# One GpSimd drain in each expert unit of the second MoE, behind the unit's last gather from the result

## The chip, the cores and the metric

The kernel runs on one core of a Trainium2 chip. The metric is the device time in microseconds (us) of one execution; lower is better. The engines are named as in the profile: PE (TensorE), DVE (VectorE), ACT (ScalarE), POOL (GpSimd) and SP (SyncE). An engine's name with a q behind it (POOLq, SPq) is that engine's instruction sequencer, which handles semaphores, branches, drains and the issue of DMAs.

## The reference

```python
def reference(**kwargs):
    ...
    attn_out = _attn_ref(**attn_kwargs)            # local window plus block summaries, (2, 8, 768, 64)
    B, H, S, D = attn_out.shape
    x = np.ascontiguousarray(attn_out.transpose(0, 2, 1, 3)).reshape(B * S, H * D)
    x = _moe_ref(x=x, **moe_kwargs)                # leaky-ReLU feed-forward, 512 -> 2048 -> 512
    return _moe2_ref(x=x, **moe2_kwargs)

def _moe2_ref(x, w_gate, w_noise, noise, w1, w2):
    ...
    top2 = np.argpartition(-noisy_logits, 2, axis=1)[:, :2]     # two of 8 experts for each of 1536 tokens
    ...
    out = np.zeros((N, D), dtype=np.float32)
    for e in range(E):
        for k in range(2):
            mask = top2[:, k] == e
            ...
            h = np.maximum(x[mask] @ w1[e], 0.0)
            out[mask] += top2_w[mask, k, None] * (h @ w2[e])
    return out.astype(np.float32)
```

## The kernel before

The program has three parts. Attention and the first feed-forward layer fill about the first 430 us; a table of planned steps sets their order. During that time the router writes, for every token and each of its two experts, a row into a table in DRAM, by scatters of single rows (L531, 24 DMAs). All of that stays as it was.

The second MoE works through nine **units**: unit 0 and unit 1 are the two halves of expert 0's 420 slots, and units 2 to 8 are experts 1 to 7 with 420 slots each, in four pieces of 105 rows. For a unit, `gather` reads the unit's rows of the table, clamps the token numbers on POOL (`gi`, L763) and fetches the tokens with one indirect DMA per piece (`xg`, L770). `xg_t` transposes them on PE (L787). `m1` and `m2` are the two matrix products, eight slices each (L800, L819). Since every token has two experts, a unit adds to what is already in the result: `gather_acc` fetches the result's present rows by indirect DMA (`ag`, L777), and `finish` multiplies the product by the gate, adds `ag` on DVE (L857) and scatters the sum back to the result (L858). All these indirect DMAs are issued by POOL. Units 0 and 1 have nothing to add to, and `gather_acc` issues nothing for them.

The loop over a unit's eight slices is software-pipelined: `gather(u + 1)` stands in slice 0, the previous unit's `finish` in slices 2 and 3, and `gather_acc(u)` at the end of slice 3. On POOL the order that results in a middle unit is: four scatters (L858), four gathers from the result (L777), the clamp for the next unit (L763), four gathers of tokens (L770), and so on. ACT and DVE have a fixed order; PE and POOL take theirs from the scheduler.

Behind the last unit stands a branch for experts that have more tokens than slots (L982 and L983), which this input does not take. Then the program's context closes: all engines drain, meet at a barrier, and the semaphores are cleared. The profile shows these closing instructions at L1019, the opening ones at L1008. At the branch's end (L983) POOL's sequencer also executes one INC_SWDGE_SEM, which brings the semaphores of its DMA queue to the values that both ways through the branch agree on.

Of the kernel before, what the change touches and what calls it, by code (L numbers as in the profile page):

```python
# [18 lines left out]
IOA = bass.IndirectOffsetOnAxis  # L19
# [101 lines left out]
def attention_moe_kernel(ctx: ExitStack, tc: tile.TileContext, q, k, v, w_in, w_out, w_gate, w_noise, noise, w1, w2,  # L121
                         const, const_bf, out):
    nc = tc.nc
# [28 lines left out]
    def load_piece(e, i):  # L152

        m, c = i // 4 + 1, i % 4
        n = 4 * m
        if c == 0:
            ew[e, m] = tuple(t.rearrange("p (c f) -> p c f", c=n) for t in pair(f"e{e}{m}", e % 2))
        hi, lo = (t.rearrange("p c f -> p (c f)")[:, c * 1024:(c + 1) * 1024] for t in ew[e, m])
        raw = spool.tile([P, 1024], F32, tag="s4", name=f"e{e}{m}{c}")
        if m == 1:  # L160
            nc.sync.dma_start(raw, w1[e, c * P:(c + 1) * P, :])
        else:
            nc.sync.dma_start(raw.rearrange("p (c f) -> p c f", c=2),
                              w2[e, c * 256:(c + 1) * 256, :].rearrange("(c p) f -> p c f", p=P))
        split(hi, lo, raw, nc.vector)
# [592 lines left out]
    def gather(u):  # L758
        e, r0, nj = units[u]
        tb = rp.tile([SLOTS, nj, 2], I32, tag="tb", bufs=3, name=f"tb{u}")  # L760
        nc.sync.dma_start(tb, tabd[e * TS + r0:e * TS + r0 + nj * SLOTS, :].rearrange("(p j) c -> p j c", j=nj))
        gi = rp.tile([SLOTS, nj], I32, tag="gi", bufs=3, name=f"gi{u}")
        nc.gpsimd.tensor_scalar(gi, tb[:, :, 0], (N if u else N - G) - 1, None, op0=ALU.min)  # L763
        if u:
            x = mp.tile([SLOTS, nj, DM], F32, tag="xg", name=f"xg{u}")
        else:
            x = pa.tile([SLOTS, nj, DM], F32, tag="qn", bufs=1, name=f"xg{u}")
        xg = [x[:, j, :] for j in range(nj)]
        for j in range(nj):
            nc.gpsimd.indirect_dma_start(out=xg[j], out_offset=None, in_=x2d if u else x2d[:N - G, :], in_offset=IOA(ap=gi[:, j:j + 1], axis=0))  # L770
        ex[u] = dict(tb=tb, gi=gi, xg=xg, e=e, nj=nj, n=nj * SLOTS)

    def gather_acc(u):
        d = ex[u]
        d["ag"] = mp.tile([SLOTS, d["nj"], DM], F32, tag="ag", name=f"ag{u}")
        for j in range(d["nj"] if d["e"] else 0):
            nc.gpsimd.indirect_dma_start(out=d["ag"][:, j, :], out_offset=None, in_=out,  # L777
                                         in_offset=IOA(ap=d["gi"][:, j:j + 1], axis=0))

    def xg_t(u, c):  # L780
        d = ex[u]
        if c == 0:
            d["x"] = [(mp if u else pa).tile([P, KD, d["n"]], F32R, tag=f"x{s}0", name=f"ex{s}{u}") for s in "hl"]
        xh, xl = d["x"]
        ps = bank("VR"[c % 2], f"xgps{u}{c}")
        for j in range(d["nj"]):
            nc.tensor.transpose(ps[:, j * SLOTS:(j + 1) * SLOTS], d["xg"][j][:, c * P:(c + 1) * P], ident[:SLOTS, :SLOTS])  # L787
        nc.scalar.activation(xh[:, c, :], ps[:, :d["n"]], AF.Copy)
        nc.vector.tensor_sub(xl[:, c, :], ps[:, :d["n"]], xh[:, c, :].bitcast(F32))

    def m1(u, f):
        d = ex[u]
        wh, wl = ew[d["e"], 1]
        xh, xl = d["x"]
        w = d["n"]
        ps = bank("H%d" % (f % 2), f"eh{u}{f}")
        n = 0
        for c in range(KD):
            for a, x in ((wh, xh), (wh, xl), (wl, xh)):
                nc.tensor.matmul(ps[:, :w], a[:, c, f * P:(f + 1) * P], x[:, c, :], start=n == 0, stop=n == 3 * KD - 1)  # L800
                n += 1
        gh, gl = ((mp if u else pa).tile([P, w], F32R, tag="g" + s, bufs=3, name=f"eg{s}{u}{f}") for s in "hl")
        nc.scalar.activation(gh, ps[:, :w], AF.Relu)  # L803
        nc.vector.scalar_tensor_tensor(gl, ps[:, :w], 0.0, gh.bitcast(F32), op0=ALU.max, op1=ALU.subtract)  # L804
        d["g", f] = (gh, gl)
# [16 lines left out]
    def out_sb(u):  # L822
        d = ex[u]
        w = d["n"]
        for i in range(2):
            y = pa.tile([P, 2, w], F32, tag=f"x{'hl'[i]}0", name=f"y{u}{i}")
            for c in (2 * i, 2 * i + 1):
                copy(i, y[:, c % 2, :], d["acc", c])
                d["y", c] = y[:, c % 2, :]
# [13 lines left out]
    def finish(u, j, rows=False):  # L843

        d = ex[u]
        if rows:
            ps = d["acc", j]
        else:
            ps = bank("VR"[j % 2], f"yps{u}{j}")
            for c in range(KD):  # L850
                nc.tensor.transpose(ps[:SLOTS, c * P:(c + 1) * P], d["y", c][:, j * SLOTS:(j + 1) * SLOTS], ident)  # L851
        y = d["ag"][:, j, :]
        gate = d["tb"][:, j, 1:2].bitcast(F32)
        if d["e"] == 0:
            nc.vector.tensor_scalar(y, ps[:SLOTS, :], gate, None, op0=ALU.mult)
        else:
            nc.vector.scalar_tensor_tensor(y, ps[:SLOTS, :], gate, y, op0=ALU.mult, op1=ALU.add)  # L857
        i = nc.gpsimd.indirect_dma_start(out=out, out_offset=IOA(ap=d["tb"][:, j, 0:1], axis=0), in_=y, in_offset=None,  # L858
                                         bounds_check=N - 1, oob_is_err=False)
        for o in d.setdefault("out", []):  # L860
            tc.declare_no_dep(i.ins, o.ins, reason="an expert has each token once")
        d["out"].append(i)
# [25 lines left out]
    def second(u, f):  # L888
        if rows[u]:
            for j in range(units[u][2]):  # L890
                m2_rows(u, f, j)
        else:
            m2(u, f)
# [13 lines left out]
    second(0, 3)  # L907
    route_end()
    gather_acc(0)
    for f in range(5, NFE):  # L910
        m1(0, f)
# [6 lines left out]
    for u in range(1, nu):  # L918
        end = u == nu - 1
        for f in range(NFE):  # L920
            m1(u, f)
            if f == 0 and not end:
                gather(u + 1)
            if units[u][0] + 1 < E and f < 7:
                load_piece(units[u][0] + 1, f)
            if f == 1 and u > 1:
                second(u - 1, NFE - 1)
                if not rows[u - 1]:
                    out_sb(u - 1)
            if f in (2, 3) and u > 1:  # L930
                for j in range(2 * f - 4, min(2 * f - 2, units[u - 1][2])):
                    finish(u - 1, j, rows[u - 1])
            if f == 3:
                gather_acc(u)
            if f == NFE - 1 and not end:
                for c in range(2):
                    xg_t(u + 1, c)
            if f >= 2 and not (end and f == NFE - 1):
                second(u, f - 2)
        if not end:  # L940
            for c in range(2, KD):
                xg_t(u + 1, c)
            if units[u][0] + 1 < E:
                load_piece(units[u][0] + 1, 7)
            second(u, NFE - 2)
# [78 lines left out]
```

## Time and profile before

| what | us |
|---|---|
| median of 3 runs (lowest, highest) | 760.88 (760.31, 761.65) |
| the profiled execution, its own time | 759.27 |
| its span, first to last instruction | 757.5 |
| its mean granted TensorE clock, as a share of 2.4 GHz | 0.978 |

The span counts the sequencers' instructions too, so opening and closing work is in it. Semaphore waits, branches, drains and the issue of DMAs are never counted as an engine's busy time.

### The profile page before, as it was taken

How to read it: one execution, taken by the hardware profiler on the slowest of the kernel's cores; microseconds unless marked ns; L12 is line 12 of the kernel's file. 1: busy time of each engine (PE TensorE's matmuls, PEld its weight loads, DVE VectorE, ACT ScalarE, POOL GpSimd, SP SyncE). 2: the span in 40 equal slices, each digit the busy share in tenths (PEclk: the TensorE clock that was granted, in tenths of full speed). 3: DMA queues.
4: the chain of work that ended last, by engine and by line, in shares of the span. 5: the costliest groups of instructions: out<-in, count | busy, mean ns of one | idle time of the engine just before them, and what ended most of it. 6: DMA issues, size and time to landing. Idle time of an engine off the chain costs nothing.

```text
span 757.5 us, 12206 instructions
## 1 busy us (share of the span) xinstructions
PE 705.0 (93%) x4581; PEld 632.7 (84%) x4581; DVE 422.6 (56%) x1035; ACT 320.1 (42%) x770; POOL 219.6 (29%) x230
## 2 busy tenths in 40 slices
PE   6779789899999999999999989999999999999990
PEld 4567678788888898888888879999999999999880
DVE  4899999965554554353575356354545455554220
ACT  4659556564544444353353244343334342433100
POOL 2545632453131021030120423233232424231320
PEclk9889999999999999999999999999999999999996
DMA  9976054453152012000353166455454645541120
GB/s 246 271 206 177 10 160 161 146 125 66 51 186 62 29 29 55 29 1 1 112 163 112 33 220 207 158 171 185 146 187 155 192 160 157 174 161 38 49 61 26
DMA packets 81821, 92.34 MB, mean 122 GB/s; under 512 B 47574, under 2 KB 57046, under 8 KB 81752
## 3 DMA queue, kind: packets, MB, share of 16 engines
q1 hardware_dynamic: 73560, 72.13, 32.0%
q0 software_dynamic: 8192, 19.33, 8.4%
q8 instruction: 38, 0.62, 0.4%
q14 instruction: 31, 0.25, 0.1%
HBM read 78.63 MB, written 13.40 MB: 121 GB/s over the span
## 4 chain that ended last, share of the span: by engine, by line
PE 76%; DVE 11%; DMA 4%; issue 3%; ACT 2%; POOL 1%; SPq 0%; POOLq 0%; DVEq 0%; ACTq 0%
PE eh L800 18%; PE eacc L819 15%; PE h L410 14%; PE acc L433 14%; PE eacc L839 4%; PE sps L329 2%; PE xgps L787 2%; PE vps L362 1%; DVE mag L607 1%; PE yps L851 1%; DVE early L608 1%; DMA raw<-in_moe_w_in_dram 1%; DVE early L609 1%; DVE raw L608 1%; DVE raw L609 1%
## 5 line engine op out<-in xcount | busy, mean ns | idle before, releaser
L803 ACT ACTIVATE egh<-eh 128x420 fp32r<-128x420 f32 (+1 forms) x72 | 34.8, 483 | 186.9 <-PE eh L800 183.2
L804 DVE SCALAR_TENSOR_TENSOR egl<-eh,egh 128x420 fp32r<-128x420 f32 (+1 forms) x72 | 39.3, 546 | 126.9 <-ACT egh L803 126.1
L414 DVE TENSOR_TENSOR lt<-h,lt 128x256 f32<-128x256 f32 x96 | 40.4, 420 | 59.5 <-ACT lt L413 58.9
L413 ACT ACTIVATE lt<-h 128x256 f32<-128x256 f32 x96 | 36.5, 381 | 69.9 <-PE h L410 68.7
L858 POOL DMA_INDIRECT out_dram<-ag,tb x32 | 31.8, 993 | 113.9 <-DVE ag L857 102.1
L410 PE MATMUL h<-xh,w0h 128*128 128x256 f32 x192 | 56.2, 296 | 5.6 <-DVE lt L414 4.8
L342 POOL TENSOR_TENSOR sm<-sm,st 128x480 f32<-128x480 f32 x24 | 24.8, 1034 | 115.4 <-DVE st L341 78.1
L410 PE MATMUL h<-xh,w16h 128*128 128x256 f32 x192 | 56.5, 294 | 0.5 <-DVE lt L414 0.5
L770 POOL DMA_INDIRECT xg<-x2d,gi x32 | 35.3, 1104 | 73.9 <-PE xgps L787 52.1
L410 PE MATMUL h<-xl,w0h 128*128 128x256 f32 x192 | 55.2, 289 | 1.4 <-DVE xl L366 1.4
L410 PE MATMUL h<-xh,w0l 128*128 128x256 f32 x192 | 55.4, 289 | 1.1 <-POOL w0l L150 1.1
L410 PE MATMUL h<-xh,w16l 128*128 128x256 f32 x192 | 54.4, 283 | 0.3 <-POOL w16l L150 0.3
L410 PE MATMUL h<-xl,w16h 128*128 128x256 f32 x192 | 54.4, 283 | 0.0
L421 ACT ACTIVATE gh<-lt 128x256 fp32r<-128x256 f32 x96 | 40.0, 416 | 33.7 <-DVE lt L414 33.2
L531 POOL DMA_INDIRECT tabd<-pl,si x24 | 23.9, 997 | 86.8 <-DVE si L527 42.6
L422 DVE TENSOR_TENSOR gl<-lt,gh 128x256 fp32r<-128x256 f32 x73 | 34.1, 467 | 21.1 <-ACT gh L421 18.7
L410 PEld LDWEIGHTS h<-xh,w0h 128*128 128x128 f32 x192 | 37.1, 194 | 8.6 <-DVE lt L414 3.4
L433 PE MATMUL acc<-w1h,gl 128*128 128x512 f32 x96 | 38.7, 405 | 2.1 <-DVE gl L422 2.1
L410 PEld LDWEIGHTS h<-xl,w0h 128*128 128x128 f32 x192 | 37.3, 195 | 3.6 <-DVE xl L366 2.1
L433 PE MATMUL acc<-w1h,gh 128*128 128x512 f32 x96 | 40.0, 417 | 0.0
L433 PE MATMUL acc<-w17h,gh 128*128 128x512 f32 x96 | 39.6, 413 | 0.0
L334 ACT ACTIVATE sm<-sm,st 128x120 f32<-128x120 f32 x96 | 36.6, 383 | 6.1 <-DVE st L332 6.0
(303 smaller groups left out, 2156.7 us busy)
## 6 DMA issues: line engine op xcount, KB each, us to landing
e<-in_moe_w_dram SPq DMA_DIRECT2D x64, 512.0 KB, 3.8
early<-in_moe_w_in_dram SPq DMA_DIRECT2D x8, 512.0 KB, 5.0
early<-in_moe_w_out_dram SPq DMA_DIRECT2D x8, 512.0 KB, 6.7
raw<-in_moe_w_in_dram SPq DMA_DIRECT2D x8, 512.0 KB, 3.7
raw<-in_moe_w_out_dram SPq DMA_DIRECT2D x8, 512.0 KB, 4.0
vw<-in_v_dram SPq DMA_DIRECT2D x20, 192.0 KB, 4.4
vn<-in_v_dram SPq DMA_DIRECT2D x8, 384.0 KB, 7.2
qn<-in_q_dram SPq DMA_DIRECT2D x12, 256.0 KB, 5.1
```

The lines of the kernel that those rows point to most:

```text
L334: nc.scalar.activation(sm[:, t, :], sm[:, t, :], AF.Exp, bias=st[:, t:t + 1], scale=-1.0, accum_out=st[:, 4 + t:5 + t])
L410: nc.tensor.matmul(ps[:, :G], a[:, c, c0:c0 + P], x[:, c, :], start=n == 0, stop=n == 3 * KD - 1)
L413: nc.scalar.activation(t, ps[:, :G], AF.Copy, scale=0.01)
L414: nc.vector.tensor_max(t, ps[:, :G], t)
L421: nc.scalar.activation(gh, t, AF.Copy)
L422: eng.tensor_sub(gl, t, gh.bitcast(F32))
L433: nc.tensor.matmul(accs[g, t], a[:, t * P:(t + 1) * P], w[:, f % 8, :], start=f == 0 and n == 0, stop=f == NF - 1 and n == 2)
L770: nc.gpsimd.indirect_dma_start(out=xg[j], out_offset=None, in_=x2d if u else x2d[:N - G, :], in_offset=IOA(ap=gi[:, j:j + 1], axis=0))
L800: nc.tensor.matmul(ps[:, :w], a[:, c, f * P:(f + 1) * P], x[:, c, :], start=n == 0, stop=n == 3 * KD - 1)
L803: nc.scalar.activation(gh, ps[:, :w], AF.Relu)
L804: nc.vector.scalar_tensor_tensor(gl, ps[:, :w], 0.0, gh.bitcast(F32), op0=ALU.max, op1=ALU.subtract)
L819: nc.tensor.matmul(ps, a[:, f, c * P:(c + 1) * P], x, start=f == 0 and n == 0, stop=f == NFE - 1 and n == 2)
```

## The change

`gather_acc` now returns its last DMA, and where there is one, a drain of POOL is placed behind it on POOL. A drain is an instruction of the sequencer; as it is written here it waits for no semaphore and increments none.

```diff
     def gather_acc(u):
         d = ex[u]
         d["ag"] = mp.tile([SLOTS, d["nj"], DM], F32, tag="ag", name=f"ag{u}")
+        i = None
         for j in range(d["nj"] if d["e"] else 0):
-            nc.gpsimd.indirect_dma_start(out=d["ag"][:, j, :], out_offset=None, in_=out,
-                                         in_offset=IOA(ap=d["gi"][:, j:j + 1], axis=0))
+            i = nc.gpsimd.indirect_dma_start(out=d["ag"][:, j, :], out_offset=None, in_=out,
+                                             in_offset=IOA(ap=d["gi"][:, j:j + 1], axis=0))
+        return i
...
             if f == 3:
-                gather_acc(u)
+                i = gather_acc(u)
+                if i is not None:
+                    with tc.issue_after(i.ins):
+                        nc.gpsimd.drain()
```

Units 2 to 8 have such a gather, so there are seven drains. Nothing else is added or removed, no instruction changes its place on any engine, and no wait changes. The listing of an engine's order leaves drains out. This is POOL's order around units 5 and 6 in the changed kernel (`ag` of units 4 and 5, `gi` and `xg` of units 6 and 7; the digits are buffer numbers):

```order
L778 DMA ag_6101<-out_dram,gi_5596 105x512 x4
L763 TENSOR_SCALAR gi_6314<-tb_6312 105x4
L770 DMA xg_6316<-x2d,gi_6314 105x512 x4
L860 DMA out_dram<-ag_6101,tb_5594 1536x512 x4
L778 DMA ag_6460<-out_dram,gi_5955 105x512 x4
L763 TENSOR_SCALAR gi_6673<-tb_6671 105x4
L770 DMA xg_6675<-x2d,gi_6673 105x512 x4
```

The rows are the same as before, but for line numbers (L778 was L777, L860 was L858). A drain stands between each L778 row and the L763 row under it. In units 7 and 8 the clamp has no further unit to serve, and the drain stands directly ahead of the next four scatters (L860).

## Rows read from the trace of the kernel before

**Rows 1.** The page: busy time, share and instructions of each engine.
```profile
PE 705.0 (93%) x4581; PEld 632.7 (84%) x4581; DVE 422.6 (56%) x1035; ACT 320.1 (42%) x770; POOL 219.6 (29%) x230
```

**Rows 2.** Windows in the second MoE, and the last 37.5 us.
```profile
core 0: us, PE busy (x) PEld busy (x) DVE busy (x) ACT busy (x) POOL busy (x), PEclk, DMA share, GB/s
...
640.00:680.00 40.00, 40.00 (x226) 39.20 (x225) 20.32 (x26) 14.35 (x23) 13.29 (x13) 1.00 0.52 173
...
720.00:757.50 37.50, 19.39 (x90) 15.21 (x88) 4.79 (x7) 1.57 (x3) 5.66 (x6) 0.83 0.14 42
```

**Rows 3.** The same columns for the last 10.5 us.
```profile
747.00:757.50 10.50, 0.00 (x0) 0.00 (x0) 0.00 (x0) 0.00 (x0) 0.00 (x0) 0.50 0.00 0
```

**Rows 4.** Line L983, GpSimd's own sequencer (POOLq): ns min/median/max, first and last start.
```profile
L983 POOLq EVENT_SEMAPHORE  x5: 17/43/43, 743.8 to 744.2; - x5
...
L983 POOLq INC_SWDGE_SEM  x1: 2560/2560/2560, 744.3 to 744.3; - x1
```

**Rows 5.** Line L1019, the closing instructions: the same columns.
```profile
L1019 POOLq EVENT_SEMAPHORE  x4: 17/17/17, 756.7 to 757.4; - x4
L1019 POOLq DRAIN  x3: 46/106/9713, 746.9 to 757.2; - x3
L1019 SPq DRAIN  x3: 7/7/13, 747.6 to 756.9; - x3
```

**Rows 6.** Line L1008, the opening instructions: the same columns.
```profile
L1008 POOLq DRAIN  x1: 176/176/176, 0.3 to 0.3; - x1
```

**Rows 7.** Waits of the SP queue from 600 us on: total, times, longest.
```profile
SPq L1019 <- PEq L1019: 9.7, 2, 9.2
```

**Rows 8.** DMA queue kinds, and issues on GpSimd's queue: count, median us to landing.
```profile
q0 software_dynamic: 8192, 19.33, 8.4%
...
xg<-x2d,gi POOLq DMA_INDIRECT x32, 4.3
out_dram<-ag,tb POOLq DMA_INDIRECT x32, 3.4
ag<-out_dram,gi POOLq DMA_INDIRECT x28, 4.0
tabd<-pl,si POOLq DMA_INDIRECT x24, 2.3
...
vsd<-vw POOLq DMA_DIRECT2D x2, 48.0 KB, 3.0
```

**Rows 9.** Timeline of GpSimd: start, us, what, idle before and its releaser.
```profile
493.47 1.04 POOL L770 DMA_INDIRECT xg<-x2d,gi  x1 [13.20 <-issue]
...
644.58 0.22 POOL L763 TENSOR_SCALAR gi<-tb 105x4 int32<-105x4 int32 x1
653.40 1.04 POOL L770 DMA_INDIRECT xg<-x2d,gi  x1 [8.60 <-PE xgps L787]
...
657.80 0.96 POOL L770 DMA_INDIRECT xg<-x2d,gi  x1 [0.30 <-issue]
667.81 0.99 POOL L858 DMA_INDIRECT out_dram<-ag,tb  x1 [9.05 <-DVE ag L857]
...
721.11 0.96 POOL L777 DMA_INDIRECT ag<-out_dram,gi  x1 [0.30 <-issue]
734.27 0.99 POOL L858 DMA_INDIRECT out_dram<-ag,tb  x1 [12.20 <-DVE ag L857]
...
740.48 0.95 POOL L858 DMA_INDIRECT out_dram<-ag,tb  x1 [1.09 <-DVE ag L857]
```

**Rows 10.** Issue to landing: lines L777, L858 (from 700 us on) and L770.
```profile
DMA to landing us min/median/max: 3.1/4.0/6.1
...
DMA to landing us min/median/max: 3.0/3.0/5.1
...
DMA to landing us min/median/max: 3.2/4.3/6.7
```

**Rows 11.** Timeline of TensorE: the next transposes of gathered tokens.
```profile
648.67 0.88 PE L787 MATMUL xgps<-cst,xg 105*128 105x105 f32 x8
```
## The prediction, as it was put on record before the change ran

> **What bounds the kernel now.** I read the windows first. PE is busy for 40.00 us of each 40 us from 480 to 720 us; the window from 640 us stands for all six [rows 2]. Over the whole span it is 93% busy, POOL 29% [rows 1]. So in the stretch where the drains go, PE alone sets the pace. A drain on POOL can take no wait away from PE there, because there is none. It can only give PE a new one.
>
> The last 37.5 us are different: PE is busy for only 19.39 us of them [rows 2]. The last counted instruction of the whole program is POOL's scatter at 740.48, 0.95 us long [rows 9], so it ends at 741.43. The span ends at 757.5. In those 16 us no engine is busy, and the chain of waits, which ends at the last busy instruction, says nothing of them. The last 10.5 us have neither busy engines nor DMA traffic: 0 GB/s [rows 3].
>
> What fills this tail has to be read from the sequencers' rows:
>
> - 741.4 to 743.8: the last scatter lands. From issue to landing it takes 3.0 us at the median of the last eight [rows 10], so until about 743.5; POOL's five semaphore waits begin at 743.8 and 744.2 [rows 4].
> - 744.3 to 746.9: one INC_SWDGE_SEM, 2.56 us [rows 4].
> - 746.9 to 756.6: one DRAIN of POOL, 9.713 us, the longest of POOL's three at L1019. It is the first of them: the first starts at 746.9, and POOL's next semaphore instruction comes at 756.7 [rows 5].
> - 756.7 to 757.5: the barrier, the clearing and two more drains of POOL, 46 and 106 ns [rows 5].
>
> Meanwhile the others wait. SP, whose own drains take 7 to 13 ns [rows 5], stands 9.2 us at the barrier; the view of waits puts this down to PEq [rows 7], but it is POOL that is missing. That one drain is on the path, and it is 1.3% of the time.
>
> **What the 9.713 us are.** Nothing moves on the DMA queues while the drain runs [rows 3], and the last transfer landed some 3 us before. So it does not wait for data. It isn't the price of a drain as such either: POOL's two later ones take 46 and 106 ns [rows 5], and the one at the program's start, behind a few small fills and no DMA, 176 ns [rows 6]. What the long one has behind it and the three short ones have not is the queue of software DMAs: 32 gathers of tokens, 32 scatters, 28 gathers from the result, 24 table scatters and 2 plain ones, 118 in all [rows 8]. No drain stands among them. I read the 9.713 us as work per DMA that the drain does for everything issued since the drain before it: 9.713 / 118 = 82 ns each, an estimate. The trace has only one such drain, so that the cost grows with the number is not shown. It is the open point of this forecast.
>
> **The change, part by part.**
>
> *The closing drain.* In POOL's order the last new drain stands behind unit 8's four gathers, and only four scatters follow it. By 82 ns each, 4 x 82 = 0.33 us are left, and with the dearer of the closing empty drains (0.106) 0.43 us. If the work goes by bytes, the last four (4 x 105 rows x 2,048 bytes = 0.86 MB of 19.33 MB [rows 8]) cost 9.713 x 0.0445 = 0.43 us. If only some 32 of the 118 were still held at the end, 304 ns each, four would leave 1.2 us. Below, the floor is an empty drain, 0.05 us. I take 0.4 us: gain 9.713 - 0.4 = **9.3 us**, all of it on the path, since the barrier waits for POOL alone; bounds 8.5 to 9.7.
>
> *The INC_SWDGE_SEM ahead of it.* 2.56 us for raising eight semaphores is long, but the trace has no second one of this kind. If it too walks through what is held, it shrinks with the closing drain. I take no change and keep a gain of up to 2.5 us as a bound.
>
> *The seven new drains.* They hold POOL's queue. The last gather from the result is in flight then; it lands 4.0 us after its issue at the median and 6.1 at most [rows 10], and its own instruction is 0.96 us long [rows 9], so a drain that waits for the landing stands 3.0 to 5.1 us. Then come the held DMAs. The first drain has 46 of them behind it (2 plain, 24 table scatters, 12 gathers of tokens, 4 scatters, 4 gathers from the result), 3.8 us; the next five 12 each, 1.0 us; the last one 8, 0.7 us. So I estimate 7 to 9 us for the first and 4 to 6 us for the others; if landing isn't waited for, 3.8 and 1.0; the floor is again 0.05.
>
> Queued behind the drain are the clamp of 0.22 us and the next gathers of tokens. In five units POOL idles between the two until PE's transposes free the buffer: 13.20 us in the first of them, 8.60 in the last, which is also the shortest of the five [rows 9]. The long estimate meets the long gap, and the others fit too. So the gathers start when they did, and the drains cost nothing on the path. In units 7 and 8 the scatters come next; in unit 8, the tighter of the two, POOL idles 12.20 us ahead of them [rows 9].
>
> If the cover is gone: suppose each drain costs the full 9.713 us whatever is held, on top of the 5.1 us, so 14.8. Then the gathers of tokens start 6.2 us later than 653.40, the last ends about 664.9 instead of 658.76, still ahead of the scatter at 667.81, and lands by 657.80 + 6.2 + 6.7 = 670.7 [rows 9, 10]. In the unit before, the same lateness meets the transposes at 648.67 [rows 11] with gathers of 40 us earlier, landed by about 631: 18 us to spare. In unit 8 the drain would end at 722.07 + 14.8 = 736.9, and four scatters, 0.99 + 0.30 = 1.29 us apart [rows 9], put the last at 740.7, 0.3 us late. So even this costs only 0.3 us.
>
> *Sum.* The profiled execution took 759.27 us; 759.27 - 9.3 = 750.0. The median of the runs shown stands 1.61 us above it; carried along, **751.6 us**.
>
> **A rule against it.** The closing row shows 9,713 ns on POOL and 7 to 13 ns on SP [rows 5]. The Trainium skill, page "VectorE: DVE Perf Modes", section "The DRAIN you can't avoid", says that the drains which the runtime puts at a program's start and end are a constant of about 12 ns on all five engines. By that page there is nothing to take away, and the time would stay at 760.9. SP's row agrees with it; POOL's row, some 800 times that constant, does not.
>
> **The rivals.**
>
> *The closing drain is a fixed price.* It may cost 9.7 us whenever software DMAs were issued at all, or for some end-of-program work that earlier drains don't spare, for instance once per ring of the queue. For it: the trace has only one drain behind DMAs, so a constant fits as well as a sum. Against it: the drain at 0.3 us and the two behind the long one are short. Then the end stays and the new drains hide, as worked out: **760.9 to 761.2**. It is also the case in which the change does nothing. Chance 0.10. (The skill's constant points the same way; it gets no chance beyond this, since its size is refuted by the row.)
>
> *A fixed part and a part per DMA.* With the fixed part between 1.5 and 8 us, the gain is 1.7 to 8 us: about 753 to 759. Nothing in the rows speaks for a split; the 46 ns drains speak against a fixed part of that size. Chance 0.07.
>
> *The last unit's drain holds the final scatters.* Unit 8's drain ends at 722.07 plus its length X, and four scatters follow at 1.29 us apart, the last of them now due at 740.48 [rows 9]. They are late once X exceeds 740.48 - 3 x 1.29 - 722.07 = 14.5 us, and then every microsecond more is one of the time, if the closing drain does not shrink. With 18 us, which needs a landing wait far above the 6.1 us that the trace shows, **764.4**. Chance 0.03.
>
> **How the numbers follow.** The forecast, 751.6 with the closing drain nearly empty, has 0.80. The range takes in its bounds: down by 0.35 for an empty drain, by 2.5 for the INC_SWDGE_SEM and a little scatter, 748.5; up by 0.8 for a dearer remnant, by 0.8 for scatter (the runs shown lie within 0.8 us of their median) and into the first part of the split case, 754. About 0.2% (1.5 us) is what a measurement of this kernel can tell from no change. Faster by more: 0.80 + 0.07 = 0.87. Within it: 0.10. Slower: 0.03.
>
> **What would show it.** Right: the closing DRAIN of POOL at about 0.4 us instead of 9.713, the span at about 748, and seven new POOLq DRAIN rows, the first clearly longer than the next five; PE still 40.00 us busy in every 40; L770 starting where it did, with POOL's idle time ahead of it shortened or the same. Wrong: a closing drain of 9 us or more with short drains before it (the price is fixed), or a gain at the end that comes back as lateness of the last scatter, past 740.48. If INC_SWDGE_SEM shrinks, the time is below 750.

## The result and the profile after

The changed kernel takes **748.64 us** (median of 4 runs, 746.75 to 750.66) against 760.60 us before (median of 4): ratio 0.9848, 95% interval 0.981 to 0.9885. In a second comparison, with 6 and 11 runs, it was 0.9845 (0.9815 to 0.9876). That is 12 us, or 1.5%.

The closing instructions are at L1024 now (L1019 before), the branch's end at L988 (L983 before). The rows of POOL's sequencer there, with minimum, median and maximum in ns, then the first and last start:

```profile
L1024 POOLq EVENT_SEMAPHORE  x4: 17/17/17, 747.1 to 747.8; - x4
L1024 POOLq DRAIN  x3: 46/106/377, 746.3 to 747.6; - x3
L1024 SPq DRAIN  x3: 7/7/13, 747.0 to 747.3; - x3
```

```profile
L988 POOLq EVENT_SEMAPHORE  x5: 17/42/43, 745.6 to 745.9; - x5
...
L988 POOLq INC_SWDGE_SEM  x1: 280/280/280, 746.0 to 746.0; - x1
```

The long drain of [rows 5] has gone from 9,713 ns to 377, while the other two are 46 and 106 ns as they were. The row to look at next is INC_SWDGE_SEM: it was 2,560 ns [rows 4] and is 280. Together the two rows give 9.34 + 2.28 = **11.62 us**, all at the end of the program.

The seven new drains stand in the middle of the second MoE:

```profile
L939 POOLq DRAIN  x7: 6151/7963/10161, 478.3 to 720.6; - x7
```

They are 6.2 to 10.2 us long. The record of each begins while its unit's earlier gathers are still being issued, so the part behind the last gather is shorter. It is read from POOL's timeline (start, us, what, idle time before it and its releaser):

```profile
471.57 0.99 POOL L860 DMA_INDIRECT out_dram<-ag,tb  x1 [7.23 <-DVE ag L857]
...
481.04 0.95 POOL L778 DMA_INDIRECT ag<-out_dram,gi  x1 [0.31 <-issue]
488.63 0.53 POOL L763 TENSOR_SCALAR gi<-tb 105x4 int32<-105x4 int32 x1 [6.64 <-issue]
495.50 1.04 POOL L770 DMA_INDIRECT xg<-x2d,gi  x1 [6.33 <-PE xgps L789]
...
645.57 0.95 POOL L778 DMA_INDIRECT ag<-out_dram,gi  x1 [0.31 <-issue]
650.98 0.22 POOL L763 TENSOR_SCALAR gi<-tb 105x4 int32<-105x4 int32 x1 [4.46 <-issue]
655.43 1.04 POOL L770 DMA_INDIRECT xg<-x2d,gi  x1 [4.23 <-PE xgps L789]
...
669.83 0.99 POOL L860 DMA_INDIRECT out_dram<-ag,tb  x1 [9.05 <-DVE ag L859]
...
723.14 0.96 POOL L778 DMA_INDIRECT ag<-out_dram,gi  x1 [0.30 <-issue]
736.29 1.00 POOL L860 DMA_INDIRECT out_dram<-ag,tb  x1 [12.19 <-DVE ag L859]
...
742.50 0.96 POOL L860 DMA_INDIRECT out_dram<-ag,tb  x1 [1.09 <-DVE ag L859]
```

From the end of the last gather to the clamp of the next unit (L763) POOL now idles 6.64 us in the first unit and 4.46 in unit 6. The gathers of tokens behind it, ahead of which POOL had idled 13.20 and 8.60 us [rows 9], now wait 6.33 and 4.23 us for PE's transposes. The idle times and the clamp add up to 13.5 and 8.9 us as before: the drain has moved into the idle time and has not lengthened it. In unit 8 POOL still waits 12.19 us for DVE ahead of its first scatter (12.20 before).

PE shows the same. Each kernel's stretch from the first gather of tokens behind the first drain to the end of the last scatter is one window (engine columns as in [rows 2]), first of the kernel before, then of the changed one:

```profile
493.47:741.43 247.96, 245.92 (x1348) 235.15 (x1347) 114.91 (x151) 77.63 (x121) 76.65 (x76) 1.00 0.44 141
```

```profile
495.50:743.46 247.96, 245.92 (x1348) 235.12 (x1346) 114.93 (x151) 77.63 (x121) 76.62 (x76) 1.00 0.44 141
```

Both are 247.96 us long with PE busy for 245.92 us. So nothing was won or lost there, and the windows of 40 us in between are full, as before:

```profile
640.00:680.00 40.00, 40.00 (x226) 39.20 (x225) 20.32 (x26) 14.33 (x22) 13.36 (x13) 1.00 0.51 167
680.00:720.00 40.00, 40.00 (x219) 37.31 (x218) 14.35 (x21) 9.82 (x17) 9.28 (x9) 1.00 0.18 56
720.00:747.90 27.90, 21.42 (x100) 17.05 (x98) 4.79 (x7) 1.57 (x3) 7.09 (x8) 0.98 0.22 64
```

The window starts 2.03 us later in the changed kernel's profiled execution (495.50 against 493.47). Its scatter at 471.57, ahead of the first drain, is late by as much. This is the same scatter before:

```profile
469.55 0.99 POOL L858 DMA_INDIRECT out_dram<-ag,tb  x1 [7.23 <-DVE ag L855]
```

So the 2 us arise before any drain, where the two programs are alike; they are spread between executions (the four runs' times differ by 3.9 us). The profiled executions therefore differ by 759.27 - 749.66 = 9.61 us, which is 11.62 less these 2.0; the medians of the runs, in which the spread evens out better, differ by 12.0.

### The profile page after: what moved, and what is told of

Its sections match the earlier page's. It is cut to its first block, busy times and chain, and to the rows that moved or that the text cites. A ratio compares the mean times of both kernels' runs of the same rounds, so it can differ in the third digit from the quotient of the medians.

```text
span 747.9 us, 12213 instructions
## 1 busy us (share of the span) xinstructions
PE 707.7 (95%) x4581; PEld 634.4 (85%) x4581; DVE 423.2 (57%) x1035; ACT 319.6 (43%) x770; POOL 220.3 (29%) x230
## 4 chain that ended last, share of the span: by engine, by line
PE 78%; DVE 10%; issue 4%; ACT 3%; DMA 3%; POOL 1%; SPq 0%; POOLq 0%; DVEq 0%; ACTq 0%
PE eh L802 18%; PE eacc L821 15%; PE acc L433 15%; PE h L410 14%; PE eacc L841 4%; PE sps L329 3%; PE xgps L789 1%; PE yps L853 1%; PE vps L362 1%; DVE raw L608 1%; DVE mag L607 1%; DVE early L609 1%; PE aps L348 1%; DVE early L608 1%; DVE raw L609 1%
## 5 line engine op out<-in xcount | busy, mean ns | idle before, releaser
L860 POOL DMA_INDIRECT out_dram<-ag,tb x32 | 31.8, 993 | 113.8 <-DVE ag L859 102.0
L770 POOL DMA_INDIRECT xg<-x2d,gi x32 | 35.4, 1105 | 51.8 <-PE xgps L789 43.2
```

## The experiments

All kernels are the changed one with the drains chosen by the unit, and for two of them something added. "Held" is the number of POOL's DMAs between the last drain ahead of the close and the closing drain, counted in POOL's order.

**One drain, in unit 8 alone** (held at the close: 4).

```diff
-                if i is not None:
+                if u == 8:
```

> One drain alone, in unit 8; 114 software DMAs are held when it stands and 4 at the close. Per-DMA theory (46 ns + 82 ns for each DMA held): the closing drain is 0.38 us and INC_SWDGE_SEM 0.28 us as with seven drains, the time within 1 us of theirs (ratio to before about 0.985); the new drain does the whole work, 9.4 to 11.4 us from the end of the last gather, and just fits into POOL's 12.2 us of idle time. Rival, each of the seven drains gives something of its own: a smaller gain, ratio about 0.997. Rival, a long drain is no longer covered: the last scatter starts more than 0.3 us late against the last product of PE.

Measured: 750.41 us, ratio 0.9857 (0.9832 to 0.9883). The closing drain and the new one:

```profile
L1024 POOLq DRAIN  x3: 46/106/383, 749.4 to 750.7; - x3
```

```profile
L939 POOLq DRAIN  x1: 12860/12860/12860, 723.3 to 723.3; - x1
```

```profile
725.85 0.95 POOL L778 DMA_INDIRECT ag<-out_dram,gi  x1 [0.31 <-issue]
739.01 0.99 POOL L860 DMA_INDIRECT out_dram<-ag,tb  x1 [12.21 <-DVE ag L859]
```

The whole work now sits in this one drain: 723.33 + 12.86 = 736.19, which is 9.39 us from the end of the last gather (726.80), and 9.39 / 114 = 82 ns for each DMA held. The last transfers are over long before; these windows split the drain at 729.1:

```profile
723.00:729.10 6.10, 6.10 (x31) 5.24 (x30) 0.59 (x1) 0.52 (x1) 2.89 (x3) 1.00 0.49 142
729.10:736.20 7.10, 7.10 (x36) 6.12 (x35) 0.59 (x1) 0.85 (x2) 0.00 (x0) 1.00 0.01 2
```

In the last 7.1 us the queues move 2 GB/s and the drain goes on. So with 114 held the landing is hidden behind the work per DMA and does not add to it (with fewer held it is otherwise, see the end of this section). The drain fits into the 12.21 us that POOL idles anyway, with 2.8 us to spare. INC_SWDGE_SEM was 280 ns here too. By the ratios the one drain is 0.7 us behind the seven, within the 1 us expected.

**One drain, in unit 2 alone** (held: 72).

> One drain alone, in unit 2; 46 DMAs are held there, 72 at the close. By number of DMAs: closing drain 0.046 + 72 x 0.082 = 5.9 us, INC_SWDGE_SEM on the line through 0.28 us (4 held) and 2.56 us (118 held), 1.64 us; gain 9.71 - 5.9 + 2.56 - 1.64 = 4.7 us, ratio about 0.994. By bytes (24 of the 46 are tiny table scatters): 72 of the 92 large ones, 7.6 us. Rival, a one-off price that any earlier drain pays: 0.4 us and the full gain.

Measured: 756.78 us, ratio 0.9954 (0.9934 to 0.9974).

```profile
L1024 POOLq DRAIN  x3: 46/106/5936, 747.1 to 753.6; - x3
```

```profile
L988 POOLq INC_SWDGE_SEM  x1: 1640/1640/1640, 745.4 to 745.4; - x1
```

5.94 and 1.64 us, the numbers of the count by DMAs; 7.6 by bytes and 0.4 by a one-off price are out. The gain in the two rows is 3.78 + 0.92 = 4.7 us, 0.6% of the time; the ratio's interval, 0.3% to 0.7%, holds it.

**One drain, in unit 5 alone** (held: 36).

> One drain alone, in unit 5; 82 DMAs are held there, 36 at the close. By number: closing drain 0.046 + 36 x 0.082 = 3.0 us, INC_SWDGE_SEM 0.92 us. By bytes: 36 of 92, 3.8 us. One-off price: 0.4 us.

```profile
L1024 POOLq DRAIN  x3: 46/106/2996, 748.3 to 751.8; - x3
```

3.00 us, and INC_SWDGE_SEM 0.920: by number again. One run, 753.99 us.

**Drains in units 2 to 7, none in unit 8** (held: 12).

> Drains in units 2 to 7, none in unit 8; 12 DMAs are held at the close. By number: closing drain 0.046 + 12 x 0.082 = 1.03 us, INC_SWDGE_SEM 0.44 us. By bytes: 12 of 92, 1.3 us. One-off price: 0.4 us.

```profile
L1024 POOLq DRAIN  x3: 46/106/1031, 746.8 to 748.4; - x3
```

1.03 us and 0.440. One run, 750.48 us.

**Twelve tiny DMAs more** (held: 24).

```diff
+    scr = dpool.tile([12, 16, 1], F32, name="scr")
...
-                if i is not None:
+                if 2 <= u <= 7:
                     with tc.issue_after(i.ins):
-                        nc.gpsimd.drain()
+                        i = nc.gpsimd.drain()
+                if u == 7:
+                    with tc.issue_after(i.ins):
+                        for n in range(12):
+                            nc.gpsimd.dma_start(scr[n], cst[:16, n:n + 1])
```

> Drains in units 2 to 7 as in the run without unit 8's, and behind unit 7's drain twelve more software DMAs of 64 bytes each (16 partitions x 4 bytes, from the constants to an unused DRAM buffer), in a gap of 21 us that POOL has there. They are added work and change no output. 24 DMAs are held at the close instead of 12. By number of DMAs: closing drain 0.046 + 24 x 0.082 = 2.0 us, 0.98 us more than without them, and INC_SWDGE_SEM 0.68 us. By bytes (768 bytes in all): as without them, about 1.0 us. By descriptors (192 against 1,260): 1.2 us.

```profile
L1029 POOLq DRAIN  x3: 46/106/2023, 746.1 to 748.7; - x3
```

2.02 us against 1.03 without them, and INC_SWDGE_SEM 0.677 against 0.440 (one run, 750.73 us). The twelve move 768 bytes and are no gathers, and cost 83 ns each at the close. So the price goes by the DMA, whatever its size; the rivals by bytes and by descriptors fall.

**A drain where it is not covered**: the seven, and an eighth directly ahead of the program's last scatter (held at the close: 1).

```diff
+        after = ExitStack()
+        if u == 8 and j == 3:
+            with tc.issue_after(d["out"][-1].ins):
+                i = nc.gpsimd.drain()
+            after.enter_context(tc.issue_after(i.ins))
         i = nc.gpsimd.indirect_dma_start(out=out, out_offset=IOA(ap=d["tb"][:, j, 0:1], axis=0), in_=y, in_offset=None,
                                          bounds_check=N - 1, oob_is_err=False)
+        after.close()
```

> The seven drains and an eighth directly ahead of the program's last scatter, where POOL has no slack. If a drain waits until the DMAs issued before it have landed: the third scatter lands 3.0 us after its issue, 2.05 us before which the last scatter was due, so the last scatter starts 1.0 to 1.5 us late; the closing drain holds one DMA, 0.13 us; the span's end comes about 1 us later than with seven drains, less than the runs scatter. If it only walks through what is held and waits for nothing: 0.3 us, inside the 1.09 us for which POOL waits for DVE, the last scatter on time.

Measured: 756.88 us (four runs from 750.47 to 757.94), ratio 0.99 (0.984 to 0.9959). The drain, and POOL's timeline around it:

```profile
L863 POOLq DRAIN  x1: 5213/5213/5213, 744.0 to 744.0; - x1
```

```profile
742.22 0.99 POOL L865 DMA_INDIRECT out_dram<-ag,tb  x1 [1.08 <-DVE ag L859]
744.29 0.96 POOL L865 DMA_INDIRECT out_dram<-ag,tb  x1 [1.09 <-DVE ag L859]
750.12 0.96 POOL L865 DMA_INDIRECT out_dram<-ag,tb  x1 [4.86 <-issue]
```

```profile
744.00:748.60 4.60, 1.26 (x6) 0.64 (x4) 0.75 (x1) 0.00 (x0) 0.96 (x1) 0.96 0.27 80
748.60:748.70 0.10, 0.00 (x0) 0.00 (x0) 0.00 (x0) 0.00 (x0) 0.00 (x0) 0.50 0.01 0
748.70:749.20 0.50, 0.00 (x0) 0.00 (x0) 0.00 (x0) 0.00 (x0) 0.00 (x0) 0.50 0.00 0
```

The other scatters follow each other by 2.07 us, so the last was due at about 746.4; it starts at 750.12, **3.8 us late**. Three DMAs are held ahead of this drain, 0.3 us by the count. It lasts until 744.04 + 5.21 = 749.25, behind the transfers of the scatter before it, which run until about 748.6 (80 GB/s, then 0), and another 0.87 us pass before the last scatter starts. The theory that it waits held, that it only walks fell. My size was too small twice over: the third scatter's transfers ended 4.3 us after its start, where I had taken the median of 3.0 in [rows 10] (in the kernel before, this very scatter is the one that took the 5.1 us there), and about 0.6 us to the drain's end and 0.9 us to the next instruction came on top. The closing drain fell to 132 ns and INC_SWDGE_SEM to 203, which gives back 0.3 us. The ratio's interval overlaps that of the seven drains, so the cost is read from the timeline and not from the time.

**The changed kernel and unit 8's drain alone, on one chip.**

> The changed kernel once more, for a narrower interval. The tail's two rows explain 9.34 us (closing drain) + 2.28 us (INC_SWDGE_SEM) = 11.6 us. If they are all there is, the ratio is 1 - 11.6 / 760.4 = 0.9847; if the drains also cost or gave something in the second MoE, it lies beside that by more than the interval.

> The kernel with unit 8's drain alone once more, on the same chip as the seven. The closing rows are the same as with seven (0.38 and 0.28 us), so the ratio is 0.985 as well, and the two medians differ by less than 2 us. If the six other drains give something, this one is slower by more.

Measured: with seven 750.93 us, ratio 0.9845 (0.9815 to 0.9876); with one 752.15 us, ratio 0.9867 (0.9836 to 0.9897). That agrees with the two rows' 11.6 us as all there is (0.9847 was expected); the interval of the seven leaves about 2.3 us either way. The medians of one and of seven differ by 1.2 us, and the ratios of the earlier runs (0.9857 and 0.9848) in the same direction, but inside the intervals; whether the other six give anything can't be told.

The closing rows of all the kernels in one table, with the line that was drawn before these runs through 46 ns and 82 ns for each DMA held, and for INC_SWDGE_SEM through 0.28 us at 4 and 2.56 at 118:

| held at the close | closing drain, us | 0.046 + 0.082 x held | INC_SWDGE_SEM, us | line |
|---|---|---|---|---|
| 1 | 0.132 | 0.13 | 0.203 | 0.22 |
| 4 | 0.377 | 0.37 | 0.280 | (0.28) |
| 12 | 1.031 | 1.03 | 0.440 | 0.44 |
| 24, of them 12 tiny | 2.023 | 2.01 | 0.677 | 0.68 |
| 36 | 2.996 | 3.00 | 0.920 | 0.92 |
| 72 | 5.936 | 5.95 | 1.640 | 1.64 |
| 118 | 9.713 | 9.72 | 2.560 | (2.56) |

**How long a drain stands while DMAs are in flight.** At the close everything has landed. The drains in the second MoE begin with gathers in flight, and the runs above show four counts. First unit 2's drain alone (46 held), then unit 5's (82 held), each with the time to landing of the last gather ahead of it:

```profile
L939 POOLq DRAIN  x1: 9188/9188/9188, 477.7 to 477.7; - x1
DMA to landing us min/median/max: 4.7/4.7/4.7
```

```profile
L939 POOLq DRAIN  x1: 10917/10917/10917, 603.4 to 603.4; - x1
DMA to landing us min/median/max: 4.2/4.2/4.2
```

The drains end at 486.90 and 614.33; these last gathers started at 480.24 and 606.60. In the same way for the two other counts:

| held | run, drain | from the last gather's end to the drain's end, us | 0.046 + 0.082 x held | from its landing to the drain's end, us |
|---|---|---|---|---|
| 12 | no drain in unit 8, unit 4's drain | 3.6 | 1.03 | 0.5 |
| 46 | unit 2's drain alone | 5.7 | 3.82 | 2.0 |
| 82 | unit 5's drain alone | 6.8 | 6.77 | 3.5 |
| 114 | unit 8's drain alone | 9.4 | 9.39 | 6.9 |

With 82 and 114 held the drain ends on the line, as if nothing were waited for. With 12 and 46 held it ends later than the line, and behind the landing by about 43 ns for each DMA held. So landing and work neither add up nor overlap fully: it looks as if about half of the 82 ns can only be done after the landing. That fits all four rows, but no run was made to test it.

## Why the prediction was right, and where its size was off

- **Where the time lies.** That PE fills the second MoE and that the tail is POOL's closing drain was right, and was seen only because the sequencers' rows were read: the chain of waits stops at the last busy instruction.
- **9.713 us as 82 ns for each of 118 DMAs.** This was the open point. Seven counts now lie on the line, and tiny DMAs cost as much as large ones. The fixed price (0.10) and the split (0.07) fell. SP's drains took 7 to 13 ns, POOL's closing drain from 132 to 9,713. The Trainium skill's page "VectorE: DVE Perf Modes", section "The DRAIN you can't avoid", gives the drains that the runtime puts at start and end a constant of about 12 ns on all five engines. If it means drains like these, which stand at the kernel's closing line, SP's rows agree with it and POOL's do not.
- **The closing drain afterwards.** 0.4 us was forecast, 0.377 measured.
- **INC_SWDGE_SEM.** This is the term that was mis-sized. I took no change and kept 2.5 us as a bound; it fell by 2.28 us. Its time goes by what is held as well, 20 ns for each DMA, so a DMA held costs 102 ns at the end in all. With this term the forecast would have been 751.6 - 2.3 = 749.3 against the 748.64 measured, and the rest is less than the spread of the runs. The measured time lies only 0.14 us above the range's lower end, which was that low because of this bound. My reason for leaving the term alone, that the trace has no second instruction of this kind, was wrong. The kernel before has one at the program's start, ahead of any DMA, and it is short, which could have raised the suspicion:

```profile
L1008 POOLq INC_SWDGE_SEM  x1: 27/27/27, 0.1 to 0.1; - x1
```

- **The seven drains cost nothing.** Right, and for the reason given: POOL's idle time in front of the gathers of tokens covers them, and PE's 245.92 us are the same. Their length behind the last gather was put at 7 to 9 us for the first drain and 4 to 6 for the others. POOL's idle time says 6.6 us for the first and 3.9 to 4.5 for the next four; the rows of the drains give 2.8 and 2.7 in units 7 and 8. I had added the landing and the whole work per DMA; in part they overlap.
- **The rival in which the last unit's drain holds the scatters.** It did not come about, but its mechanism is real: put where POOL has no slack, one drain made the last scatter 3.8 us late.

## What to carry to other kernels

Look at what follows the last busy instruction: of 16 us there, 12.3 were two sequencer instructions of GpSimd, and no view of busy engines or of the chain shows them. In every kernel here each DMA issued from GpSimd since its last drain cost 0.1 us at the end, whatever its size. One earlier drain was enough, as far as the runs can tell, since it stood late, with few DMAs behind it, and where GpSimd idled for longer than the drain took. On the path a drain costs the landing it waits for, 3.8 us here.

## What the runs showed of the hardware that was not expected

- The INC_SWDGE_SEM at the branch's end took 0.20 to 2.56 us, by the number of DMAs that POOL had issued since its last drain (table above).
- POOL's drain waits for DMAs in flight, not for its own engine alone: with 3, 12 and 46 held it ended only behind the last transfer, with 3 held although 0.3 us of work would have done. The drain ahead of the last scatter outlasted POOL's last instruction (744.29 + 0.96 = 745.25) by 4.0 us, and the transfers by about 0.6 us. The Trainium skill's page "PSUM — Partial Sum Buffer", section "Engine vs sequencer instructions", says that a drain waits for the engine to go fully idle; here it stood for longer than that.
- The first of the seven drains, with 46 DMAs held, kept POOL idle for 6.64 us where 46 x 0.082 = 3.8 us would do by the line. The same count in unit 2's drain alone gave 5.7 us from the last gather's end, of which 2.0 lie behind the landing. Open: whether about half of the work per DMA has to wait for the landing, as the four counts suggest.
